# First layer pair of an MLP by Strassen's scheme for both batches, with the orders of two engines written out

## The chip, the cores and the metric

The kernel runs on one core of one Trainium2 chip. The metric is the device time of one execution in microseconds (us), as the median of the runs shown. PE is the matrix engine, DVE the vector engine, ACT the scalar engine, POOL the GpSimd engine, SP the engine that issues transfers.

## The reference

Clustered attention (2 batches, 8 heads, 768 rows of 64) feeds two MLPs, all in float32 on 1536 rows of 512:

```python
mask = q_assign[:, :, :, None] == k_assign[:, :, None, :]
scores = np.where(mask, scale * q @ k.T, -1e9)      # per head
attn = softmax(scores) ; x = attn @ v               # (2*768, 512)
h = x @ w_in ; g = h * sigmoid(h) ; x = g @ w_out   # MLP 1, d_ff 2048
gate = sigmoid(x @ w_gate) ; val = x @ w_val        # MLP 2, d_ff 1536
out = (gate * val) @ w_out
```

The weights come in as 64-bit floats and are converted in the kernel.

## The kernel before, in words

Attention goes through eight pairs of heads, four for each batch. For each pair PE forms the scores of 12 tiles of 128 rows, DVE takes their maxima, ACT the exponentials, PE transposes them and multiplies them by the values (`values`, L551). The last pair ends in `finish_last` (L630, L637): PE spreads the reciprocal denominators over the rows by matmuls with the identity, DVE multiplies them into the values and writes the quarter of the activations `acc`. For each batch `acc` has four quarters: b11 and b12 are ready before the last pairs, b21 and b22 only when the last pair's first and second half are finished.

MLP 1 works in eight pairs of 128-wide column blocks of `w_in` (`hidden`), each followed by its output product (`mixed`). A pair with four quarters of the activations is a 2x2 block product, done by Strassen's scheme in Winograd's form (`strassen`): seven products, named x, X, y, z, w, v, W, in place of eight. Their right operands are the quarters b11, b21, b22 and the sums t1 = b12 - b11, t2 = b22 - t1, t3 = b22 - b12, t4 = t2 - b21. X goes on in the PSUM bank of x, W in that of w; the difference d is read from w's bank before W goes on there. A product is KQ x 3 = 6 matmuls for a batch, since each float32 operand is split into a rounded high part (ACT, L65) and a low part (a subtraction, on DVE or POOL, L81 and L1003), and three of the four combinations are kept.

For the first pair the batches go apart. Batch 0 uses the scheme, its operands having been made long before. Batch 1 is done without it: `direct` forms eight products, 2 times 24 matmuls (L1013), from the four quarters. Its sums t1 to t4, which the later pairs need, are made after that (`right_sums`, `right_last`), while PE does the first output products.

The weights are converted in three DVE passes a chunk (L778, L780, L782; two, L775 and L782, where the lowest bits are kept too), with ACT before and POOL after them; a pair of input weights is two chunks, and POOL then builds the sums s1 to s4 (L827 to L830) and low parts (L807). The lists `behind` and `paced` hold instructions behind which the next passes (DVE) or the next copies (ACT) are queued.

What sets the order: a scheduler orders every engine's queue at build time. `tc.manual_schedule` makes the named engines take the traced order; around the first pair this holds for PE alone, so DVE's and ACT's orders there are the scheduler's. `tc.issue_after(ins)` puts the instructions of the block that are on `ins`'s own engine behind `ins` in its queue; it adds no wait between engines.

Of the kernel before, what the change touches and what calls it, by code (L numbers as in the profile page):

```python
# [32 lines left out]
def clustered_attention_then_two_mlps(ctx, tc, qT, kT, v, cen, cenT, w1i, w1o, w2g, w2v, w2o, out):  # L33
# [26 lines left out]
    copied, latest, moved, firsts, added = [], [], [], [], []  # L60
# [28 lines left out]
    def right_sums(temporary, name, b, caster, adder, kept):  # L89

        put = partial(right_operand, name, b, caster=caster, subber=adder)
        b11, b21, b12, b22 = quarters(b).values()
        t1 = temporary(f"{name}t1{b}")
        adder.tensor_tensor(t1, b12, b11, op=ALU.subtract)
        kept[b] = t1
        t2 = temporary(f"{name}t2{b}")
        adder.tensor_tensor(t2, b22, t1, op=ALU.subtract)
        put("t2", t2)
        yield
        t4 = temporary(f"{name}t4{b}")  # L100
        adder.tensor_tensor(t4, t2, b21, op=ALU.subtract)
        put("t4", t4)
        yield
        t3 = temporary(f"{name}t3{b}")
        adder.tensor_tensor(t3, b22, b12, op=ALU.subtract)
        put("t3", t3)
        yield

    def scheme_operands(temporary, name, b, caster, adder):
# [4 lines left out]
        def minus(n, x, y):  # L114
            sums[n] = temporary(f"{name}t{n}{b}")
            adder.tensor_tensor(sums[n], x, y, op=ALU.subtract)
# [20 lines left out]

    def right_last(name, b, src, caster, subber):
        right_operand(name, b, "t1", src, caster, subber)

    rp = ctx.enter_context(tc.tile_pool(name="rp", bufs=2))
    with ExitStack() as att:
# [404 lines left out]
        def values(p, j, g):  # L547
            vv = heads[p][4]
            o = ps_v.tile([P, G], F32, tag="v", name=f"v{p}_{j}_{g}")
            for n, kt in enumerate((4, 5, 0, 1, 2, 3)):  # L550
                m = nc.tensor.matmul(  # L551
                    o[(L, U)[kt % 2]],
                    lhsT=vv[:, j, kt, :],
                    rhs=ring[:, kt, g * G : (g + 1) * G],
                    start=n < 2,
                    stop=n >= NT - 2,
                )
            main, rest = (L, U) if j == 0 else (U, L)
            other = wk.tile([P, G], F32, tag="other", name=f"other{p}_{j}_{g}", bufs=1)
            ends[:] = [nc.scalar.activation(other[main], o[rest], AF.Copy), m]  # L560
            if p not in xf:
                xf[p] = fin.tile([P, S], F32, tag="xf", name=f"xf{p}")
            nc.vector.tensor_tensor(xf[p][main, g * G : (g + 1) * G], o[main], other[main], op=ALU.add)  # L563
# [54 lines left out]
        def finish_last(h):  # L618
# [9 lines left out]
            for j, r in enumerate((L, U)):  # L628
                for i in range(n):
                    nc.tensor.matmul(  # L630
# [5 lines left out]
                    )  # L636
            nc.vector.tensor_tensor(  # L637
                acc[:, hp, h, b, :], xf[p][:, h * HS : (h + 1) * HS], rb[:, 0:HS], op=ALU.mult
# [91 lines left out]
    up = ctx.enter_context(tc.tile_pool(name="up", bufs=8))  # L730
    home[1, "t1"] = ctx.enter_context(tc.tile_pool(name="tu", bufs=1))
# [135 lines left out]
    coming, ready = {}, {}  # L867

# [63 lines left out]
    def temporary(name):  # L932
        return up.tile([P, 2, HS], F32, tag="u", name=name)
# [3 lines left out]
    def strassen(w, name, take, bs, order="xyzwXvW"):  # L937

        def run(o, a, q, start=True):
            for k in range(KQ):  # L940
                for n, (s, t) in enumerate(((0, 0), (0, 1), (1, 0))):
                    for b in range(B)[bs]:
                        nc.tensor.matmul(  # L943
# [6 lines left out]
                        )  # L950
# [54 lines left out]
    def direct(w, name, take, b):  # L1005

        for m in range(2):
            o = bank(f"{name}_{b}{m}", (ppa, ppb)[m])
            for h in range(2):
                for r in range(2):  # L1010
                    for k in range(KQ):
                        for n, (s, t) in enumerate(((0, 0), (0, 1), (1, 0))):
                            nc.tensor.matmul(  # L1013
                                o[:, h, 0:HS],
                                lhsT=w[f"a{m + 1}{r + 1}"][s][:, k, :],
                                rhs=right[b, f"{r + 1}{h + 1}"][t][:, k, :],
                                start=r == 0 and k == 0 and n == 0,
                                stop=r == 1 and k == KQ - 1 and n == 2,
                            )
            take(o[:, :, 0:HS], m, b)  # L1020
            yield
# [9 lines left out]
    def hidden_directly(i, b):  # L1031
        def take(c, m, b):
            g = temporary(f"g{i}_{m}_{b}")
            nc.scalar.activation(g, c, AF.Silu)
            split(g, m, (slice(0, 2), b), f"a{i}", nc.vector)

        yield from direct(weights("1i", i), f"p{i}", take, b)
# [36 lines left out]
    def gated(i, bs, together=False):  # L1074
        gates = {}

        def gate(c, m, h, bs, inside):
            g = c if inside else temporary(f"g2{i}_{m}{h}{bs.start}")[:, bs]
# [3 lines left out]
        def value(c, m, h, bs, inside):  # L1082
# [7 lines left out]
            if together:  # L1090
                late[m, h] = parts
# [123 lines left out]
    kept = {}  # L1215
    ACT, DVE, POOL = nc.scalar, nc.vector, nc.gpsimd

    def sums(name, b):
        return right_sums(temporary, name, b, ACT, DVE, kept)

    def last(name, b):
        right_last(name, b, kept.pop(b), ACT, DVE)
# [18 lines left out]
    run(following)  # L1241
    weights("1o", 0, 1)
    rest = sums("x", 1)
    next(rest)
    with tc.issue_after(parted[0].ins):
        run(rest)
    last("x", 1)
    run(mixed(0, 0))
    run(mixed(0, 1))
    run(hidden(1, ALL))  # L1250
    for i in range(2, N1):
        following = hidden(i, ALL) if i < N1 - 1 else hidden(i, ONE[0], "xyzXwvW")
        steps(following, n=2 if i < N1 - 1 else 5)
        run(mixed(i - 1, first=int(i == N1 - 1)))
# [7 lines left out]
    zero, one = (scheme_operands(temporary, "y", b, ACT, DVE) for b in range(B))  # L1262
# [14 lines left out]
    subs = []  # L1277

    def rounding(m, h):
        late.pop((m, h))(subs)  # L1280

    def splitting():
        subs.pop(0)()

    def split_now(m, h):
        late.pop((m, h))()

# [4 lines left out]
    rounding(0, 0)  # L1292
    go(n=2)
    splitting()
# [9 lines left out]
    rounding(1, 0)  # L1304
    go(n=1)
    splitting()
    split_now(1, 1)
    go(n=1)
    rounding(0, 1)
    one("21")  # L1310
    splitting()
# [15 lines left out]
    rounding(0, 0)  # L1327
    go(n=2)
    splitting()
# [5 lines left out]
    rounding(1, 0)  # L1335
    go(n=1)
    splitting()
    split_now(1, 1)
    go(n=1)
    split_now(0, 1)  # L1340
# [81 lines left out]
```

## Time and profile before

| | |
|---|---|
| time, median of 3 runs | 768.25 us (767.39 to 768.47) |
| the profiled execution, its own time | 767.51 us |
| its span, first to last instruction | 765.7 us |
| busy in the span: PE, DVE, ACT, POOL | 755.2, 597.7, 425.9, 389.7 us |
| granted clock of PE | 1.000 of full speed |

The span is the time from the first to the last instruction on the core; the execution's own time is 1.8 us longer. Where a matmul's row gives a time, its end is modelled, and neighbouring rows overlap; the distance between starts tells the pace.

### The profile page before, as it was taken

To read this page: it belongs to the slowest core of one execution; us is meant where nothing else is said; L and a number is where in the kernel's file an instruction comes from. 1 tells how busy PE (TensorE), PEld (TensorE's weight loads), DVE (VectorE), ACT (ScalarE), POOL (GpSimd) and SP (SyncE) were. 2 spreads that over 40 slices of the span, in tenths; PEclk is the share of its full clock that TensorE was granted. 3 is DMA by queue.
4 is the path that set the end of the run, shared out by engine and by line. 5 is a ranking of instruction groups with operands and counts; after the bars stand their busy time and mean duration, and the time that the engine had idled before them with its cause. 6 is when DMAs were issued, how large, how long until landed. Compare 5 with 4: busy or idle time off the path is not lost.

```text
span 765.7 us, 11470 instructions
## 1 busy us (share of the span) xinstructions
PE 755.2 (99%) x4289; PEld 648.9 (85%) x4290; DVE 597.7 (78%) x773; ACT 425.9 (56%) x742; POOL 389.7 (51%) x361
## 2 busy tenths in 40 slices
PE   8999999999999999999999999999999999999997
PEld 4766776677767998998989989999999989999896
DVE  7887887788788968798978587986697767859566
ACT  6777776776886762534615545565544525353320
POOL 5235134644655773566647456125776745565430
PEclk9999999999999999999999999999999999999999
DMA  7677457447122122132222120010313112111104
GB/s 209 168 210 192 115 151 195 117 128 193 45 77 72 66 83 83 41 125 83 83 83 73 66 82 1 29 56 27 110 56 108 58 55 97 68 57 56 55 1 166
DMA packets 25488, 71.61 MB, mean 94 GB/s; under 512 B 4484, under 2 KB 4952, under 8 KB 25432
## 3 DMA queue, kind: packets, MB, share of 16 engines
q1 hardware_dynamic: 24888, 70.84, 30.7%
q8 instruction: 34, 0.56, 0.3%
q14 instruction: 22, 0.18, 0.1%
q10 hardware_dynamic: 544, 0.03, 0.0%
HBM read 48.01 MB, written 3.19 MB: 67 GB/s over the span
## 4 chain that ended last, share of the span: by engine, by line
PE 92%; DVE 3%; ACT 2%; DMA 1%; issue 1%; POOL 0%; SPq 0%; ACTq 0%
PE z L1134 13%; PE s L501 8%; PE v L551 7%; PE t L538 5%; PE y L1064 4%; PE h_0w L943 4%; PE h_0x L943 4%; PE v_0x L943 3%; PE g_0w L943 3%; PE g_0x L943 3%; PE v_0w L943 3%; PE y_00None L1064 2%; PE y_21None L1064 2%; PE y_20None L1064 2%; PE y_11None L1064 2%; PE y_10None L1064 2%
## 5 line engine op out<-in xcount | busy, mean ns | idle before, releaser
L514 ACT ACTIVATE e<-s,nm 128x768 f32<-128x768 f32 x96 | 86.5, 901 | 33.8 <-DVE nm L509 32.7
L509 DVE TENSOR_REDUCE nm<-s 128x1 f32<-128x768 f32 x96 | 91.4, 953 | 10.3 <-PE s L501 8.6
L1134 PE MATMUL z<-wu,ghb 128*128 128x512 f32 (+1 forms) x292 | 89.1, 387 | 0.0
L551 PE MATMUL v<-ph,vv 128*64 128x384 f32 x384 | 69.0, 495 | 0.1
L1134 PEld LDWEIGHTS z<-wu,ghb 128*128 128x128 f32 x292 | 54.5, 188 | 10.8
L501 PE MATMUL s<-ka,qa 128*128 128x384 f32 x192 | 57.5, 380 | 2.0 <-ACT e L514 1.5
L538 PE MATMUL t<-ident,e 128*128 128x128 f32 x384 | 58.4, 275 | 0.1
L1134 PE MATMUL z<-wu,glb 128*128 128x512 f32 (+1 forms) x146 | 56.7, 388 | 0.0
L538 PEld LDWEIGHTS t<-ident,e 128*128 128x128 f32 x384 | 44.9, 140 | 11.3 <-issue 9.0
L551 PEld LDWEIGHTS v<-ph,vv 128*64 128x64 f32 x384 | 24.7, 136 | 32.7 <-issue 29.0
L501 PE MATMUL s<-k,q 128*128 128x384 f32 x192 | 49.6, 339 | 0.0
L65 ACT ACTIVATE ph<-t 128x512 f32<-128x512 f32 x68 | 40.6, 598 | 12.6 <-PE t L538 12.0
L1043 DVE TENSOR_TENSOR acc<-z,acc 128x1024 f32<-128x1024 f32 x24 | 29.2, 1221 | 21.6 <-PE z L1134 21.6
L68 DVE COPY ph<-u 128x512 f32<-128x512 f32 x48 | 32.7, 682 | 16.3 <-PE u L528 16.3
L582 POOL TENSOR_TENSOR acc<-xf,rb 128x768 f32<-128x768 f32 x7 | 12.9, 1837 | 59.2 <-DMA rb<-d_rb 56.5
L807 POOL TENSOR_TENSOR wu<-cu,wu 128x512 fp32r<-128x512 f32 x12 | 16.3, 1356 | 52.0 <-ACT wu L65 52.0
L807 POOL TENSOR_TENSOR wo<-co,wo 128x512 fp32r<-128x512 f32 x16 | 24.1, 1510 | 33.5 <-ACT wo L65 33.4
L501 PEld LDWEIGHTS s<-k,q 128*128 128x128 f32 x192 | 34.5, 188 | 0.5 <-DMA k<-rows 0.3
L501 PEld LDWEIGHTS s<-ka,qa 128*128 128x128 f32 x192 | 28.9, 190 | 6.9 <-ACT e L514 5.9
L1064 PE MATMUL y<-gha,wo 128*128 128x384 f32 x128 | 32.8, 334 | 0.0
L1134 PEld LDWEIGHTS z<-wu,glb 128*128 128x128 f32 x146 | 27.4, 188 | 6.0 <-DVE glb L1003 0.5
L563 DVE TENSOR_TENSOR xf<-v,other 64x384 f32<-64x384 f32 x32 | 17.7, 553 | 14.8 <-ACT other L560 14.3
(709 smaller groups left out, 2151.9 us busy)
## 6 DMA issues: line engine op xcount, KB each, us to landing
ri<-in_w1i SPq DMA_DIRECT2D x16, 512.0 KB, 3.2
ro<-in_w1o SPq DMA_DIRECT2D x16, 512.0 KB, 3.1
ka<-kh SPq DMA_DIRECT2D x32, 192.0 KB, 3.6
rg<-in_w2g SPq DMA_DIRECT2D x12, 512.0 KB, 3.6
rv<-in_w2v SPq DMA_DIRECT2D x12, 512.0 KB, 3.1
ru<-in_w2o SPq DMA_DIRECT2D x12, 512.0 KB, 3.2
qq<-in_qT SPq DMA_DIRECT2D x8, 384.0 KB, 3.6
kk<-in_kT SPq DMA_DIRECT2D x8, 384.0 KB, 4.1
```

The source lines that it names most:

```text
L65: return nc.scalar.activation(o, i, AF.Copy)
L68: return nc.vector.tensor_copy(o, i)
L501: nc.tensor.matmul(s[:, g, 0:HS], lhsT=a[:, j, i * P : (i + 1) * P], rhs=c[:, j, g * HS : (g + 1) * HS], start=n == 0, stop=n == 1,)
L509: maxima.append(nc.vector.tensor_reduce(nm, s[:, :, 0:HS], axis=AX.XY, op=ALU.max, negate=True))
L514: x = nc.scalar.activation(e, s[:, :, 0:HS], AF.Exp, bias=nm, scale=1.0, accum_out=tots[p][:, n : n + 1])
L538: nc.tensor.transpose(t[:, kt, :], e[:, kt * P : (kt + 1) * P], ident)
L551: m = nc.tensor.matmul(o[(L, U)[kt % 2]], lhsT=vv[:, j, kt, :], rhs=ring[:, kt, g * G : (g + 1) * G], start=n < 2, stop=n >= NT - 2,)
L807: nc.gpsimd.tensor_tensor(lo, src, hi, op=ALU.subtract)
L943: nc.tensor.matmul(o[:, b, 0:HS], lhsT=w[a][s][:, k, :], rhs=right[b, q][t][:, k, :], start=start and k == 0 and n == 0, stop=k == KQ - 1 ...
L1043: added.append(nc.vector.tensor_tensor(z if to is None else to, o, z, op=ALU.add))
L1064: nc.tensor.matmul(o[:, d, 0:width], lhsT=s[:, d, k, :], rhs=t[:, c], start=k == 0 and m == 0, stop=k == 1 and m == 2,)
L1134: nc.tensor.matmul(o[:, a, c], lhsT=s[:, q * P : (q + 1) * P], rhs=r[:, c], start=k == 0 and m == 0, stop=k == 1 and m == 2, skip_group_ch ...
```

## The change

1. `finish_last` and `values` of the last pair: the queue of PE becomes value, denominators, value, denominators; the second value's PSUM tile comes from another pool (`ps_t`). The rounding of the first output weights is queued behind ACT's last copy of the ring (`drained`) and no longer behind the Silu table's load.
2. The first pair's batch 1 goes through `hidden(0, ONE[1], "xXyzwvW", True)`: seven products. `direct`, `hidden_directly`, `right_sums` and `right_last` go. The sums t1 to t4 of batch 1 are made by `scheme_operands`, between the products of batch 0. DVE's and ACT's orders are written out from batch 0's w to the last split of batch 1. The low parts of batch 0's hidden values are all on DVE and stand behind batch 1's products x to w; batch 1's (1, 1) quarter stays on POOL. Quarter 12 of batch 1 is no longer rounded. The DVE passes of pair 1's input weights are queued behind the last low part of batch 0 and behind batch 1's sum of v.
3. The first four DVE passes of the gate's weights are queued behind the last pair's sum of w (`sum_of_w`, the difference d of `hidden(7, ONE[0])`).
4. The pool of temporaries has seven shared buffers and one that only t1 and the values of X use (`own`).

```diff
-        for g in range(2):
-            values(p, 1, g)
-            if g == 0:
-                with tc.issue_after(ends[0].ins):
-                    moved[:] = [nc.scalar.activation(ex, unit[:, 0:1], AF.Silu)]
-            finish_last(g)
+        drained[:] = moved
+        values(p, 1, 0)
+        with tc.issue_after(ends[0].ins):
+            moved[:] = [nc.scalar.activation(ex, unit[:, 0:1], AF.Silu)]
+        with tc.issue_after(ends[1].ins):
+            finish_last(0)
+        with tc.issue_after(product[0].ins):
+            values(p, 1, 1, ps_t)
+        with tc.issue_after(ends[1].ins):
+            finish_last(1)
+        ends[1] = product[0]
...
+    own = ctx.enter_context(tc.tile_pool(name="own", bufs=1))
-    up = ctx.enter_context(tc.tile_pool(name="up", bufs=8))
-    home[1, "t1"] = ctx.enter_context(tc.tile_pool(name="tu", bufs=1))
+    up = ctx.enter_context(tc.tile_pool(name="up", bufs=7))
+    home[1, "21"] = ctx.enter_context(tc.tile_pool(name="tu", bufs=1))
...
-            job(("1o", i, e), plain, w1o[i, e], f"o{i}_{e}", () if i else moved)
+            job(("1o", i, e), plain, w1o[i, e], f"o{i}_{e}", () if i else (drained, moved)[e])
...
+                if c == place["2g", 0]:
+                    behind.extend(sum_of_w * 4)
...
-    def hidden(i, bs, order="xyzwXvW"):
+    def hidden(i, bs, order="xyzwXvW", apart=False):
         def take(c, m, h, bs, inside):
-            g = c if inside else temporary(f"g{i}_{m}{h}{bs.start}")[:, bs]
+            g = c if inside else temporary(f"g{i}_{m}{h}{bs.start}", own if i or bs.start else None)[:, bs]
             nc.scalar.activation(g, c, AF.Silu)
-            split(g, m, (h, bs), f"a{i}", nc.gpsimd if m and h else nc.vector)
+            helped = m and h and not (apart and bs.start == 0)
+            parts = partial(split, g, m, (h, bs), f"a{i}", nc.gpsimd if helped else nc.vector)
+            if apart:
+                late[bs.start, m, h] = parts
+            else:
+                parts()
...
-    for q in ("11", "12"):
-        right_quarter("x", 1, q, POOL, POOL)
-    for q in ("21", "22"):
-        right_quarter("x", 1, q, ACT, DVE)
-    front = hidden(0, ONE[0], "xwXyzvW")
-    steps(front, n=1)
+    right_quarter("x", 1, "11", POOL, POOL)
+    one = scheme_operands(temporary, own, "x", 1, ACT, DVE)
+    with tc.issue_after(finished[0].ins):
+        one("T1")
+    zeroth = partial(steps, hidden(0, ONE[0], "xwXyzvW", True))
+    zeroth(n=1)
     look[0] = AHEAD
     weights("1i", 0)
-    steps(front, n=5)
-    following = hidden_directly(0, 1)
-    next(following)
-    run(front)
-    run(following)
+    order.__exit__(None, None, None)
+    order = tc.manual_schedule(engines={mybir.EngineType.PE, mybir.EngineType.DVE, mybir.EngineType.Activation})
+    order.__enter__()
...
+    first = partial(steps, hidden(0, ONE[1], "xXyzwvW", True))
+    zeroth(n=1)
+    with tc.issue_after(ends[0].ins):
+        one("+21")
+    one("T2", "T3", "+t2", "+t3")
+    zeroth(n=1)
+    one("+t1", "21", "t2")
+    zeroth(n=1)
+    one("t3")
+    rounding(0, 0, 0)
+    zeroth(n=1)
+    one("t1")
+    first(n=1)
+    one("+22")
+    rounding(0, 1, 1)
+    zeroth(n=1)
+    one("T4", "+t4")
+    rounding(0, 1, 0)
+    paced.extend(rounded * 2)
+    zeroth(n=1)
+    one("t4")
+    rounding(0, 0, 1)
+    first(n=2)
+    one("22")
+    rounding(1, 0, 0)
+    first(n=2)
+    splitting(0, 0, 0)
+    splitting(0, 1, 0)
+    splitting(0, 0, 1)
+    splitting(0, 1, 1)
+    behind.extend(parted * 3)
+    first(n=1)
+    behind.extend(critical[-1:] * 3)
+    rounding(1, 1, 1)
+    first(n=1)
+    rounding(1, 1, 0)
+    rounding(1, 0, 1)
+    splitting(1, 0, 0)
+    splitting(1, 1, 1)
+    splitting(1, 1, 0)
+    splitting(1, 0, 1)
+    order.__exit__(None, None, None)
+    order = tc.manual_schedule(engines={mybir.EngineType.PE})
+    order.__enter__()
     weights("1o", 0, 1)
-    rest = sums("x", 1)
-    next(rest)
-    with tc.issue_after(parted[0].ins):
-        run(rest)
-    last("x", 1)
-    run(mixed(0, 0))
+    outs = mixed(0, 0)
+    with tc.issue_after(product[0].ins):
+        next(outs)
+    run(outs)
...
         steps(following, n=2 if i < N1 - 1 else 5)
+        if i == N1 - 1:
+            sum_of_w[:] = critical[-1:]
```

`one("T2")` makes a sum on DVE, `one("+t2")` its rounding on ACT, `one("t2")` its low part on DVE; `rounding(b, m, h)` is the rounding of a quarter of batch b's hidden values on ACT, `splitting` its low part.

## Rows read from the trace of the kernel before

**Rows 1.** the page's first part: busy us, share of the span, instructions

```profile
PE 755.2 (99%) x4289; PEld 648.9 (85%) x4290; DVE 597.7 (78%) x773; ACT 425.9 (56%) x742; POOL 389.7 (51%) x361
```

**Rows 2.** busy time by stage; columns: window, us, then busy us (instructions) by engine

```profile
238.20:253.20 15.00, 15.00 (x86) 14.58 (x85) 12.07 (x19) 10.23 (x19) 8.47 (x9) 1.00 0.21 71
```

**Rows 3.** PE's instructions in order of time: start us, us, line, out<-in, xcount

```profile
232.28 2.16 PE L551 MATMUL v<-ph,vv 128*64 128x384 f32 x12
234.27 1.75 PE L630 MATMUL rb<-ident,rs 128*64 128x128 f32 x24
236.14 2.16 PE L551 MATMUL v<-ph,vv 128*64 128x384 f32 x12
238.23 1.33 PE L943 MATMUL h_0w<-xt,wi0s 128*128 128x384 f32 x6
...
242.71 1.32 PE L943 MATMUL h_0v<-xt,wi0b 128*128 128x384 f32 x6
243.87 4.32 PE L1013 MATMUL p<-x,wi0a 128*128 128x384 f32 x24
...
249.07 4.32 PE L1013 MATMUL p<-x,wi0b 128*128 128x384 f32 x24
253.23 0.33 PE L1064 MATMUL y<-gha,wo 128*128 128x384 f32 x1
```

**Rows 4.** DVE in the same view; in brackets the idle time before an instruction

```profile
233.12 1.64 DVE L780 SCALAR_TENSOR_TENSOR co<-ro,co 128x512 int32<-128x512 int32 x1
...
235.53 0.56 DVE L563 TENSOR_TENSOR xf<-v,other 64x384 f32<-64x384 f32 x1
...
238.86 0.56 DVE L563 TENSOR_TENSOR xf<-v,other 64x384 f32<-64x384 f32 x1 [2.12 <-ACT other L560]
239.46 0.55 DVE L637 TENSOR_TENSOR acc<-xf,rb 128x384 f32<-128x384 f32 x1
...
242.91 0.95 DVE L81 TENSOR_TENSOR x<-acc,x 128x768 fp32r<-128x768 f32 x1
243.78 0.55 DVE L957 TENSOR_TENSOR h_0u<-h_0z,h_0u 128x384 f32<-128x384 f32 x1
244.25 0.55 DVE L1003 TENSOR_TENSOR gla<-g,gha 128x384 fp32r<-128x384 f32 x1
244.71 0.68 DVE L780 SCALAR_TENSOR_TENSOR ci<-ri,ci 128x512 int32<-128x512 int32 x1
...
247.78 1.18 DVE L782 SCALAR_TENSOR_TENSOR ci<-ri,ci 128x512 int32<-128x512 int32 x1
```

**Rows 5.** ACT in the same view

```profile
238.34 0.48 ACT L560 ACTIVATE other<-v 64x384 f32<-64x384 f32 x1 [0.76 <-PE v L551]
```

**Rows 6.** POOL in the same view

```profile
232.75 1.46 POOL L807 TENSOR_TENSOR wi0t<-si,wi0t 128x512 fp32r<-128x512 f32 x1
237.14 2.53 POOL L807 TENSOR_TENSOR wo<-co,wo 128x512 fp32r<-128x512 f32 x2 [2.93 <-ACT wo L65]
...
247.40 1.02 POOL L1003 TENSOR_TENSOR gla<-h_0d,gha 128x384 fp32r<-128x384 f32 x1 [6.21 <-ACT gha L65]
...
259.65 1.74 POOL L807 TENSOR_TENSOR wi1t<-si,wi1t 128x512 fp32r<-128x512 f32 x1
```

**Rows 7.** PE in the same view, MLP 1's pair 1

```profile
272.09 2.24 PE L943 MATMUL h_0y<-xt,wi1s 128*128 128x384 f32 x12
```

**Rows 8.** PE in the same view, MLP 1's last pair

```profile
443.46 1.20 PE L943 MATMUL h_0w<-xt,wi7s 128*128 128x384 f32 x6
445.09 0.50 PE L1064 MATMUL y_00None<-gha,wo 128*128 128x512 f32 x1 [0.43 <-DVE h_0u L957]
```

**Rows 9.** DVE in the same view, MLP 1's last pair and the output product

```profile
442.06 0.92 DVE L775 SCALAR_TENSOR_TENSOR cg<-cg,rg 128x512 int32<-128x512 int32 x1
...
444.49 0.55 DVE L957 TENSOR_TENSOR h_0u<-h_0y,h_0u 128x384 f32<-128x384 f32 x1
...
459.03 1.23 DVE L1043 TENSOR_TENSOR acc<-y_20None,acc 128x1024 f32<-128x1024 f32 x1 [1.50 <-PE y_20None L1064]
```

More of the change, by code (lines that the diff above doesn't have):

```diff
@@ L59, in clustered_attention_then_two_mlps @@
     maxima = []
-    copied, latest, moved, firsts, added = [], [], [], [], []
+    copied, latest, moved, drained, firsts, added, finished, product = [], [], [], [], [], [], [], []
     home = {0: xp}
@@ L87, in right_quarter, with scheme_operands @@
         right_operand(name, b, q, quarters(b)[q], caster, subber, "t1" if q == "12" else None)
[L89 to L109, printed above, removed]
+    def scheme_operands(temporary, own, name, b, caster, adder):
         b11, b21, b12, b22 = quarters(b).values()
@@ L114, in minus @@
         def minus(n, x, y):
-            sums[n] = temporary(f"{name}t{n}{b}")
+            sums[n] = temporary(f"{name}t{n}{b}", own if n == "t1" else None)
             adder.tensor_tensor(sums[n], x, y, op=ALU.subtract)
@@ L629, in finish_last @@
                 for i in range(n):
-                    nc.tensor.matmul(
+                    product[:] = [nc.tensor.matmul(
                         rb[r, i * P : (i + 1) * P],
@@ L867, in clustered_attention_then_two_mlps @@
     coming, ready = {}, {}
+    sum_of_w = []
     def come(*key, apart=False):
@@ L942, in run @@
                     for b in range(B)[bs]:
-                        nc.tensor.matmul(
+                        product[:] = [nc.tensor.matmul(
                             o[:, b, 0:HS],
@@ L1003, in split @@
         parted[:] = [subber.tensor_tensor(lo, src, hi, op=ALU.subtract)]
[L1005 to L1021, printed above, removed]
-    def hidden(i, bs, order="xyzwXvW"):
+    def hidden(i, bs, order="xyzwXvW", apart=False):
         def take(c, m, h, bs, inside):
-            g = c if inside else temporary(f"g{i}_{m}{h}{bs.start}")[:, bs]
+            g = c if inside else temporary(f"g{i}_{m}{h}{bs.start}", own if i or bs.start else None)[:, bs]
             nc.scalar.activation(g, c, AF.Silu)
-            split(g, m, (h, bs), f"a{i}", nc.gpsimd if m and h else nc.vector)
-        yield from strassen(weights("1i", i), f"h{i}", take, bs, order)
[L1031 to L1037, printed above, removed]
+            helped = m and h and not (apart and bs.start == 0)
+            parts = partial(split, g, m, (h, bs), f"a{i}", nc.gpsimd if helped else nc.vector)
+            if apart:
+                late[bs.start, m, h] = parts
+            else:
+                parts()
+        yield from strassen(weights("1i", i), f"h{i}", take, bs, order)
     def accumulate(z, o, first, to=None):
@@ L1077, in gate @@
         def gate(c, m, h, bs, inside):
-            g = c if inside else temporary(f"g2{i}_{m}{h}{bs.start}")[:, bs]
+            g = c if inside else temporary(f"g2{i}_{m}{h}{bs.start}", own if i else None)[:, bs]
             nc.scalar.activation(g, c, AF.Sigmoid)
@@ L1090, in value @@
             if together:
-                late[m, h] = parts
+                late[bs.start, m, h] = parts
             else:
@@ new lines, in splitting @@
+    def splitting(*key):
+        if key not in subs:
+            rounding(*key)
+        parted[:] = [subs.pop(key)[0]()]
+    first = partial(steps, hidden(0, ONE[1], "xXyzwvW", True))
[14 more added lines that the diff above has]
+    zeroth(n=1)
@@ L1261, in clustered_attention_then_two_mlps @@
     order.__enter__()
-    zero, one = (scheme_operands(temporary, "y", b, ACT, DVE) for b in range(B))
+    zero, one = (scheme_operands(temporary, own, "y", b, ACT, DVE) for b in range(B))
     rest = mixed(N1 - 1, 1)
@@ L1291, in clustered_attention_then_two_mlps @@
     parted_weights("2o", 0, 0)
-    rounding(0, 0)
+    rounding(0, 0, 0)
     go(n=2)
-    splitting()
+    splitting(0, 0, 0)
     zero("22")
@@ L1303, in clustered_attention_then_two_mlps @@
     go(n=4)
-    rounding(1, 0)
+    rounding(0, 1, 0)
     go(n=1)
-    splitting()
-    split_now(1, 1)
+    splitting(0, 1, 0)
+    splitting(0, 1, 1)
     go(n=1)
-    rounding(0, 1)
+    rounding(0, 0, 1)
     one("21")
-    splitting()
+    splitting(0, 0, 1)
     outs = out_of(0)
@@ L1326, in clustered_attention_then_two_mlps @@
     one("+22")
-    rounding(0, 0)
+    rounding(1, 0, 0)
     go(n=2)
-    splitting()
+    splitting(1, 0, 0)
     one("t4")
@@ L1334, in clustered_attention_then_two_mlps @@
     go(n=4)
-    rounding(1, 0)
+    rounding(1, 1, 0)
     go(n=1)
-    splitting()
-    split_now(1, 1)
+    splitting(1, 1, 0)
+    splitting(1, 1, 1)
     go(n=1)
-    split_now(0, 1)
+    splitting(1, 0, 1)
     critical.append(parted[0])
```

38 lines of the change are left out of this document (16 added, 22 removed).

## Prediction

> **What bounds the kernel now.** I read the engine totals first: the matrix engine is busy for 755.2 of 765.7 us [rows 1], so only its own instructions, and the moments in which it waits, can move the time. Then the table of the stretch that is rewritten, 238.2 to 253.2 us: PE 15.00 of 15.00 us busy, vector engine (DVE) 12.07 of 15.00 [rows 2]. PE has no gap there, but DVE has only 3 us to spare, and it has to take on new work. Next the matmuls one after the other [rows 3], then what feeds them on DVE [rows 4], ACT [rows 5] and POOL [rows 6], and last the one wait that PE shows between 262 us and the end phase, at 445 us [rows 8].
>
> Two readings are used throughout. A busy PE is not PE at its pace: 24 matmuls of 384 columns run from 249.07 to 253.23, 4.16 us, so one takes 0.173 us and a set of six (one of Strassen's products for one batch) 1.04 us. A set that starts after a wait takes 1.16 (242.71 to 243.87) [rows 3]: a wait costs its length and 0.12 more. And on DVE two independent instructions overlap by 0.09: a 768-wide subtraction shows 0.95, but the next starts 0.87 after it (242.91 to 243.78) [rows 4]; a 384-wide one shows 0.55, so 0.46. Where one needs the other, it starts 0.04 after the other's end.
>
> **Attention's end.** The order was value, both groups of denominators, value; it becomes value, denominators, value, denominators. The 24 records of the denominators start at 234.27; their row lasts 1.75 with about 0.27 for the last one, so one is issued each (1.75 - 0.27) / 23 = 0.064 us and the 24 are through at 235.8. The second value starts only at 236.14, because the one PSUM buffer is empty when DVE's addition ends, 235.53 + 0.56 = 236.09 [rows 3, 4]. In the new order the second value has another buffer. A value takes 1.99 (232.28 to 234.27). So: 234.27 + 12 x 0.064 = 235.04, second value until 237.1, 0.77 for the second denominators, the set w at 237.95 instead of 238.23: 0.3 us gained. The last quarter of the activations, b22, ended at 239.46 + 0.55 = 240.01 [rows 4]. Now the denominators end last, near 238.0; ACT's copy of half a value (0.48 [rows 5]) and DVE's addition (0.56 [rows 4]) follow the value's end at 237.2 to 238.4, and DVE's product ends near 239.0.
>
> **Seven products in place of eight.** Batch 1 of the first pair had 2 x 24 = 48 matmuls and gets 7 x 6 = 42: 6 x 0.173 = 1.04 us less on PE. From w to the first matmul of the output product PE went through 14 sets in 253.23 - 238.23 = 15.00 us, 14 x 1.04 = 14.56 and 0.44 of waits. With 13 sets and no wait the output product would start at 237.95 + 13.52 = 251.5.
>
> **What DVE has to do for it.** The sums t1 to t4 of batch 1 stood after 253 us, where nobody waited. Now they stand between. DVE's order is written out; I walk it with the durations above. T1 needs only old quarters and fits between DVE's product at 236.7 and the second value: DVE was idle for 2.12 us there [rows 4]. From 239.0: T2 until 239.95, T3 240.8, low part of 21 241.7, of t2 242.55, y's sum 243.05, low part of t3 243.9, z's sum 244.4, difference d 244.95. PE meanwhile: w 237.95, X 239.0, y 240.0, z 241.1, batch 1's x 242.15, v 243.3, and W would start at 244.35. But W goes on in the bank that d is read from, so it waits until 245.0: 0.65 + 0.12 lost. Further on DVE: low part of t1 245.85, v's sum 246.3, T4 247.15, W's sum 247.65. The low part of t4 needs ACT's rounding of T4, which stands behind three other ACT instructions and ends near 248.3, so 249.3; y's sum of batch 1 249.8, low part of 22 250.65, z's sum 251.1, d 251.7. PE: X 246.2, y 247.2, z 248.25, w 249.3, v 250.35, and its W, which waits for that d in the same way, at 251.75 rather than 251.4: 0.35 + 0.12 lost. It ends at 252.9, and the output product starts there (its first low part on DVE ends at 252.2). **0.3 us gained over 253.23**, where PE alone would give 1.7. Of the 1.4 lost, 1.24 are these two waits and the rest a short wait of batch 1's x for its bank.
>
> A price that could differ is DVE beside POOL. DVE's pass at 233.12 took 1.64 us while POOL computed a low part (232.75, 1.46) [rows 4, 6]; the same kind of pass took 0.68 at 244.71. Up to 247.4 POOL was idle for 6.2 us [rows 6], so the new sums mostly run alone; at the ends they may meet POOL's low part of the output weights and its clamps of the next pair's weights. Bounds: nothing, or one such loss at either end, 2 x 0.95 less what the waits absorb, so up to 1.2; I take nothing, since the subtractions of 242.91 and 244.25 us stood at 0.95 and 0.55 with POOL idle [rows 4].
> The Trainium skill ("SBUF — State Buffer", "Who interferes with whom") says that a DVE instruction with two SBUF inputs and a GpSimd instruction that reads SBUF exclude each other, the later one being blocked until the first ends. The 1.64 us pass agrees: it ended 0.55 after POOL's instruction. By that rule T1, if it comes second to POOL's low part (1.26 us each), would be up to 1.3 later, and the sum below would lose as much.
>
> **What moves behind it.** The six DVE passes of pair 1's input weights are tied behind the last split of batch 0 and behind batch 1's v sum. The last one ended at 247.78 + 1.18 = 248.96; now four splits end near 253.6, the six passes of about 0.5 us each follow with two sums of batch 1 between them, so near 258 at the latest. Behind it POOL builds Strassen's sums: the low part of s1 and s2 ended at 259.65, where the last one starts, so 10.7 us after the passes [rows 4, 6]. It is wanted at 272.09 by pair 1's product y [rows 7], at 271.8 after the change. From 258 it ends at 268.7, 3 us early: no cost. ACT's two copies for these weights follow a rounding of batch 0 and delay no set. POOL's dropped rounding of quarter 12, one rounding of output weights ahead of the Silu table, the buffers (seven shared and one own in place of eight) cost nothing: each has a reader several us later.
>
> **Gate's passes.** At 445.09 PE waited 0.43 us for DVE's sum of y, 444.49 + 0.55 = 445.04, which stood behind two passes of the gate's weights (the first of them at 442.06, 0.92) [rows 8, 9]. With the passes behind the sum of w, y's sum ends near 443.5, and the product starts when the set at 443.46 is through, 444.5: 0.43 of waiting and 0.12 of refill, 0.55. The passes then run between the output product's additions, where DVE is idle for 1.5 us at a time [rows 9]; the gate's weights are wanted 40 us later.
>
> **Sum.** 0.3 + 0.55 = 0.85 us less than the profiled execution's 767.51 (span 765.7), 766.65. The median of the runs shown is 768.25, 0.74 above that execution, so 767.4. About 0.2%, 1.5 us, is what a measurement of this kernel can tell from no change.
>
> **Rivals.**
> *DVE is not late.* If b22 comes earlier or the sums overlap more, PE alone sets the start, 251.5 to 251.9: 1.7 to 1.35 gained, with the gate 2.25 to 1.9: 766.0 to 766.3. For it: two waits of half a microsecond hang on a chain of eight DVE instructions. Against it: DVE's 12 us of work stood in 15 already. 0.28.
> *DVE is later still.* T1 falls behind the second value (0.95), or meets POOL at both ends (1.2): most of it reaches W, so 0.1 to 0.6 more than before in all, 768.4 to 768.9. 0.17.
> *Pair 1's weights come late; slower.* If the last DVE pass ends after 261.1 (271.8 - 10.7), PE waits at pair 1's second product, a microsecond for each. Six passes beside POOL at 1.2 to 1.6 us, queued behind four more splits, would end near 265: 3.9 lost, 771.3. Against it: DVE's sums that filled 253 to 266 are gone. 0.10.
> *The change does not bite at 445 us*, since another DVE instruction takes the passes' place: 768.0, inside the forecast's own range.
>
> **How the numbers follow.** Forecast 0.45 (767.0 to 768.0), rivals 0.28, 0.17, 0.10. Faster by over 0.2% (below 766.7): the first rival and a sliver of the forecast, 0.31. Slower (above 769.8): the third, 0.10 and a little of the second, 0.11. Within: 0.58. The range goes from the first rival's end to the second's, 765.9 to 769.0.
>
> **What would show it.** In the profile after: batch 1's W of the first pair with a wait on d, as batch 0's W; the output product starting at 252.9; no wait at the seventh output product. Wrong would be a gap ahead of pair 1's second product, or PE without any wait from 238 to 252.

## The result and the profile after

The changed kernel takes 772.31 us (median of 6 runs, 771.71 to 772.88) beside 768.25 (6 runs, 767.39 to 768.75): a ratio of 1.0054, 95% interval 1.0041 to 1.0067. It is slower by 4.1 us, and outside the range. The profiled execution took 771.71, its span 769.9, 4.2 more than before; PE is busy for 755.8 us, as before [rows 1]. Landmarks of PE place the 4.2:

| stretch | before | after | difference |
|---|---|---|---|
| first instruction to the first product x of MLP 1 | 230.63 | 231.21 | +0.58 |
| x to the first output product | 22.60 | 23.95 | +1.35 |
| from there to pair 2's x | 31.34 | 31.21 | -0.13 |
| pair 2's x to its z | 20.52 | 23.84 | +3.32 |
| from there to the last pair's first output product | 140.00 | 139.41 | -0.59 |
| from there to the end | | | -0.33 |

The first line moves without the change: among the experiments on the kernel before, the same x stood at 230.73 to 231.58. The table of PE's waits after the change (us in total, times, longest) names the rest:

```profile
PE h_0y L933 <- POOL wi2s L794: 2.3, 1, 2.3
...
PE h_1x L933 <- ACT g L998: 0.7, 1, 0.7
...
PE h_0w L933 <- DVE h_0d L947: 0.5, 1, 0.5
...
PE h_1w L933 <- DVE h_1d L947: 0.3, 1, 0.3
PE h_0y L933 <- DVE acc L618: 0.3, 1, 0.3
...
PE y_20None L1033 <- DVE acc L1012: 0.3, 1, 0.3
```

The wait of 445 us [rows 8] is gone and four waits stand in the first pair (0.7, 0.5, 0.3, 0.3). The largest wait, for POOL's `wi2s`, belongs to pair 2: no step of the prediction looked at it. The first pair in PE's order of time (start us, us, line, out<-in, xcount, idle before and its releaser), which answers to [rows 3]:

```profile
238.49 1.31 PE L933 MATMUL h_0w<-xt,wi0s 128*128 128x384 f32 x6
...
241.15 1.33 PE L933 MATMUL h_0y<-xt,wi0s 128*128 128x384 f32 x6 [0.30 <-DVE acc L618]
...
244.26 1.31 PE L933 MATMUL h_1x<-x,wi0a 128*128 128x384 f32 x6 [0.73 <-ACT g L998]
...
247.14 1.34 PE L933 MATMUL h_0w<-x,wi0t 128*128 128x384 f32 x6 [0.52 <-DVE h_0d L947]
...
254.00 1.32 PE L933 MATMUL h_1w<-x,wi0t 128*128 128x384 f32 x6 [0.32 <-DVE h_1d L947]
255.16 0.34 PE L1033 MATMUL y<-gha,wo 128*128 128x384 f32 x1
```

What feeds it, DVE and then POOL:

```profile
235.33 1.64 DVE L769 SCALAR_TENSOR_TENSOR co<-ro,co 128x512 int32<-128x512 int32 x1
237.01 0.56 DVE L543 TENSOR_TENSOR xf<-v,other 64x384 f32<-64x384 f32 x1
237.67 0.55 DVE L618 TENSOR_TENSOR acc<-xf,rb 128x384 f32<-128x384 f32 x1
238.14 1.70 DVE L96 TENSOR_TENSOR xtt<-acc 128x768 f32<-128x768 f32 x1
239.88 0.56 DVE L543 TENSOR_TENSOR xf<-v,other 64x384 f32<-64x384 f32 x1
240.54 0.55 DVE L618 TENSOR_TENSOR acc<-xf,rb 128x384 f32<-128x384 f32 x1
```

```profile
234.71 1.72 POOL L794 TENSOR_TENSOR wo<-co,wo 128x512 fp32r<-128x512 f32 x1
237.75 1.28 POOL L794 TENSOR_TENSOR wo<-co,wo 128x512 fp32r<-128x512 f32 x1 [1.33 <-ACT wo L65]
```

Two DVE instructions run beside POOL's two low parts and take 1.64 and 1.70 us: the third pass (L769) and T1 (L96). In [rows 4] a subtraction of T1's size took 0.95, and the same pass of before took 0.71:

```profile
234.79 0.71 DVE L782 SCALAR_TENSOR_TENSOR co<-ro,co 128x512 int32<-128x512 int32 x1
```

T1 stands ahead of the last quarter's addition and product in DVE's queue, so the last quarter is ready at 241.09. The walk had it near 239.0, which is 239.6 in this execution, whose x is 0.58 later: 1.5 us late.

The wait at pair 2, from its loads on. The loads of raw weights, of before and then of after (start us of the first, us):

```profile
246.87 2.49 SPq L756 DMA_DIRECT2D ro<-in_w1o  x2
264.61 5.58 SPq L756 DMA_DIRECT2D ri<-in_w1i  x2
```

```profile
260.58 0.93 SPq L743 DMA_DIRECT2D ro<-in_w1o  x2
270.20 4.19 SPq L743 DMA_DIRECT2D ri<-in_w1i  x2
```

There are two raw buffers, and a load starts when the last DVE pass over the chunk before has left one: before, the pass at 246.12 ended at 246.80 and the load came at 246.87; after, the passes of L769 from 259.82 free it for 260.58. That load is of output weights, 13.7 us later than before. Pair 2's input weights use the buffers after them: their load is 5.6 us later, 3.8 when the 1.8 us later x of pair 2 is taken off. At the end of that chain POOL makes the low part wi2s (POOL's order of time, before and then after), and PE's product y of after waits for it (third fence):

```profile
284.06 1.32 POOL L807 TENSOR_TENSOR wi2s<-si,wi2s 128x512 fp32r<-128x512 f32 x1
```

```profile
290.47 1.27 POOL L794 TENSOR_TENSOR wi2s<-si,wi2s 128x512 fp32r<-128x512 f32 x1
```

```profile
288.56 0.96 PE L933 MATMUL h_0y<-xt,wi2s 128*128 128x384 f32 x4
291.79 1.66 PE L933 MATMUL h_0y<-xt,wi2s 128*128 128x384 f32 x8 [2.27 <-POOL wi2s L794]
```

Before, wi2s ended at 285.38 and y began one set of twelve (2.08) behind x (284.57), at 286.65, so 1.27 us later. The first four matmuls of y (0.69) use the rounded high part alone, as the third fence shows: only the fifth waits for the low part. So the slack was 1.96 us. After, wi2s ended 5.37 behind x instead of 0.81: 4.56 later, 2.60 more than the slack, and y's fifth matmul started 2.65 late. The 4.56 are 3.2 by which the last pass over these weights ended later, and 1.3 that POOL lost behind it, as two of its instructions there (at 286.38 and 288.39) took 1.46 and 1.43 beside DVE, and 0.75 each before. Each weight buffer's reader has its own slack, and this one was not looked up.

### The profile page after: what moved, and what is told of

Read it like the earlier page. It is cut to its first block, busy times and chain, and to the rows that moved or that the text cites. A ratio compares the mean times of both kernels' runs of the same rounds, so it can differ in the third digit from the quotient of the medians.

```text
span 769.9 us, 11472 instructions
## 1 busy us (share of the span) xinstructions
PE 755.8 (98%) x4283; PEld 648.2 (84%) x4284; DVE 603.0 (78%) x780; ACT 428.3 (56%) x747; POOL 381.8 (50%) x359
## 4 chain that ended last, share of the span: by engine, by line
PE 88%; DVE 5%; ACT 3%; issue 2%; POOL 1%; DMA 1%; SPq 0%; DVEq 0%; ACTq 0%; POOLq 0%
PE z L1103 13%; PE s L478 8%; PE v L531 7%; PE t L515 5%; PE y L1033 4%; PE v_0x L933 3%; PE g_0w L933 3%; PE g_0x L933 3%; PE h_0w L933 3%; PE v_0w L933 3%; PE h_0x L933 3%; PE y_20None L1033 2%; PE y_21None L1033 2%; PE y_00None L1033 2%; PE y_11None L1033 2%; PE y_10None L1033 2%
## 5 line engine op out<-in xcount | busy, mean ns | idle before, releaser
L794 POOL TENSOR_TENSOR wo<-co,wo 128x512 fp32r<-128x512 f32 x16 | 22.2, 1390 | 22.4 <-ACT wo L65 22.4
```

What stands on the lines that cost most here:

```text
L794: nc.gpsimd.tensor_tensor(lo, src, hi, op=ALU.subtract)
```

## The experiments

All times beside runs of the kernel before on the same chip (767.96 to 768.37 in the medians). "Behind x" is the time from the first x of MLP 1 to the first output product: 22.60 before, 23.95 after.

**The parts alone.** The gate's passes behind the sum of w, on the kernel before:

```diff
+                if c == place["2g", 0]:
+                    behind.extend(sum_of_w * 4)
...
+        if i == N1 - 1:
+            sum_of_w[:] = critical[-1:]
```

> The kernel before with part 3 alone: the first four DVE passes of the gate's weights are queued behind the last pair's sum of w. Theory: the wait of 0.43 us at the seventh output product goes, with its refill 0.55 us, and nothing else changes: 767.7 us. Rival: the passes only move the wait to a later instruction (the gate's weights or a bank of the output product): 768.2 to 768.6 us.

767.06 us, 0.9987 (0.9978 to 0.9995). The median is 1.3 us below the kernel before where 0.55 was expected; the interval reaches from 0.4 to 1.7. In the profiled execution the span is 0.7 shorter, 0.59 of it in the stretch with the gate's passes. The first pair is as before; the last pair's output product follows its set on PE without a wait, which was 0.43 us in [rows 8]:

```profile
443.59 1.20 PE L946 MATMUL h_0w<-xt,wi7s 128*128 128x384 f32 x6
444.63 0.39 PE L1067 MATMUL y_00None<-gha,wo 128*128 128x512 f32 x1
```

The reverse, the changed kernel without that tie:

```diff
-                    behind.extend(sum_of_w * 4)
```

> The changed kernel without part 3. Theory: the wait at the seventh output product is back, 0.55 us more than the changed kernel: 772.9 us. Rival: part 3 gives nothing here because its passes stand in the way later (the changed kernel waits 0.3 us for an addition at an output product): 772.3 us.

772.88, 1.006 (1.0047 to 1.0074). The 0.4 us wait is back, and from pair 2's z to the last pair's first output product it is 140.02, where the changed kernel has 139.41. In the traces part 3 does what was forecast, in both directions; the medians alone don't tell 0.6 us apart.

Attention's end alone (part 1), on the kernel before:

```diff
+        drained[:] = moved
+        values(p, 1, 0)
...
+        with tc.issue_after(product[0].ins):
+            values(p, 1, 1, ps_t)
...
+            job(("1o", i, e), plain, w1o[i, e], f"o{i}_{e}", () if i else (drained, moved)[e])
```

> The kernel before with part 1 alone: value, denominators, value, denominators at attention's end and the earlier rounding of the first output weights. Theory: the set w of the first pair starts 0.3 us earlier after batch 0's x than before (7.3 us behind it instead of 7.6), 767.9 to 768.0 us. Rival: the reordering is a part of the loss, since the set x started 0.58 us later in the changed kernel: 768.6 us or more.

769.12, 1.0013 (1.0004 to 1.0022). The set w starts 7.25 behind x instead of 7.60, the 0.3 us forecast, and the output product 23.86 behind it. On DVE:

```profile
235.83 1.64 DVE L790 SCALAR_TENSOR_TENSOR co<-ro,co 128x512 int32<-128x512 int32 x1
...
242.24 0.96 DVE L81 TENSOR_TENSOR x<-acc,x 128x768 fp32r<-128x768 f32 x1 [2.23 <-ACT x L65]
243.12 0.42 DVE L786 TENSOR_SCALAR ci<-ci 128x512 int32<-128x512 int32 x1
243.45 0.95 DVE L81 TENSOR_TENSOR x<-acc,x 128x768 fp32r<-128x768 f32 x1
244.32 0.55 DVE L965 TENSOR_TENSOR h_0u<-h_0y,h_0u 128x384 f32<-128x384 f32 x1
```

PE's product v waits 1.6 us for that last sum. The expectation was missed and its rival (768.6 or more) came. Two causes were open: the pass beside POOL's low part (the earlier rounding moved POOL there), and the scheduler's new order, in which y's sum stands behind two low parts and a pass. Before, it stood right behind the first low part, ahead of the second one (rows left out of [rows 4]):

```profile
241.23 0.96 DVE L81 TENSOR_TENSOR x<-acc,x 128x768 fp32r<-128x768 f32 x1 [1.22 <-ACT x L65]
242.11 0.55 DVE L957 TENSOR_TENSOR h_0u<-h_0y,h_0u 128x384 f32<-128x384 f32 x1
```

So part 1 without the earlier rounding, together with part 3:

```diff
-            job(("1o", i, e), plain, w1o[i, e], f"o{i}_{e}", () if i else (drained, moved)[e])
+            job(("1o", i, e), plain, w1o[i, e], f"o{i}_{e}", () if i else moved)
```

> The kernel before with the new order at attention's end (without the earlier rounding of output weights, so POOL's first low part of them stays behind the Silu table) and with the gate's passes behind the sum of w. If the 1.64 us pass beside POOL was the whole loss of the end alone: that pass takes 0.71 again, the raw buffer is refilled 0.93 us earlier, ACT doesn't wait for the load, and y's sum is 1.0 earlier; v still waits some 0.65 us, since the order of DVE's queue is that of the end alone (low part, pass, low part, then y's sum): output product 22.85 behind x instead of 23.86, and with the gate 768.0. If the new order itself gains its 0.3 us: 22.3 behind x, 767.3. If the queue's order is the loss and not the pass: 23.8, 768.9.

767.77, 0.9996 (0.9986 to 1.0005); 23.39 behind x. On DVE:

```profile
235.70 0.69 DVE L790 SCALAR_TENSOR_TENSOR co<-ro,co 128x512 int32<-128x512 int32 x1
...
243.70 0.55 DVE L968 TENSOR_TENSOR h_0u<-h_0y,h_0u 128x384 f32<-128x384 f32 x1
```

The pass is short again, and the wait of v falls from 1.64 to 1.14 only: 0.5 us is the pass. The rest goes with the order of DVE's queue, which is argued from the rows: the new attention end with the old DVE order was not tried. None of the three places expected for the output product (22.85, 22.3 and 23.8) was met.

**The first pair.** T1 of batch 1 on POOL, at 205 us, in the changed kernel:

```diff
-    with tc.issue_after(finished[0].ins):
-        one("T1")
+    one("T1")
...
-            adder.tensor_tensor(sums[n], x, y, op=ALU.subtract)
+            (nc.gpsimd if name == "x" and n == "t1" else adder).tensor_tensor(sums[n], x, y, op=ALU.subtract)
```

> The changed kernel with the sum T1 computed by POOL, right behind quarter 11's rounding and some 25 us earlier, so that DVE doesn't meet POOL's second low part with it. Theory (the stage's loss is DVE blocked beside POOL; T1 took 1.70 us in place of 0.95 and stood ahead of the second half's product): the output product starts 22.3 us behind batch 0's x in place of 23.95, pair 2's wait of 2.3 us stays, 770.7 us. Rival (the chain of DVE's sums is too long by itself, T1 or not): 23.5 us or more behind x, 772 us.

770.58, 1.0032 (1.0019 to 1.0044); 22.51 behind x, 1.44 earlier than the changed kernel. On DVE:

```profile
235.12 1.65 DVE L769 SCALAR_TENSOR_TENSOR co<-ro,co 128x512 int32<-128x512 int32 x1
...
238.23 0.56 DVE L543 TENSOR_TENSOR xf<-v,other 64x384 f32<-64x384 f32 x1 [0.21 <-ACT other L540]
238.89 0.55 DVE L618 TENSOR_TENSOR acc<-xf,rb 128x384 f32<-128x384 f32 x1
```

The pass still takes 1.65, but with T1 away, its own 0.95 included, the last quarter follows the copy of its value; the waits of 0.73 and 0.30 are gone, and those for d stay (0.52, 0.34). The other half of the collision, the earlier rounding given up:

```diff
-            job(("1o", i, e), plain, w1o[i, e], f"o{i}_{e}", () if i else (drained, moved)[e])
+            job(("1o", i, e), plain, w1o[i, e], f"o{i}_{e}", () if i else moved)
```

> The changed kernel with both roundings of the first output weights behind the Silu table, as before, so that POOL's first low part comes some 2 us later. Theory: DVE's third pass at 235 us takes 0.7 again in place of 1.64 and the first half's product is 0.9 us earlier, but both low parts then stand beside T1 and T2, so most of it is lost again: the output product 23.5 to 24 us behind x, 772 to 772.4 us. Rival (the early rounding is the whole loss of the stage): 22.5 us behind x, 770.9 us.

772.35, 1.0052 (1.0038 to 1.0066); 23.22 behind x. POOL's low parts move to 237.59; the pass takes 0.69 and T1 0.95, at 237.03, but now T2 (239.83) meets POOL. On DVE:

```profile
235.17 0.69 DVE L769 SCALAR_TENSOR_TENSOR co<-ro,co 128x512 int32<-128x512 int32 x1
...
237.03 0.95 DVE L96 TENSOR_TENSOR xtt<-acc 128x768 f32<-128x768 f32 x1
...
239.83 1.36 DVE L96 TENSOR_TENSOR xtt<-acc,xtt 128x768 f32<-128x768 f32 x1
```

The 0.73 won in the first pair don't show in the time: pair 2's wait stayed, and in the profiled execution the clock fell behind it (last section).

**Pair 2's weights.** The passes of pair 1's input weights without their ties:

```diff
-    paced.extend(rounded * 2)
...
-    behind.extend(parted * 3)
...
-    behind.extend(critical[-1:] * 3)
```

> The changed kernel without the ties of pair 1's weights: their two ACT copies and six DVE passes are queued where the scheduler puts them, five of the passes ahead of batch 1's sum of y. Theory (late weights cost 2.4 us at pair 2's product y, because each later load waits for a buffer that pair 1's passes free): that wait goes, and the six passes, some 3 us of DVE's time, make the output product start 1.5 to 3 us later; 771.5 to 773 us in all. Rival (the 2.3 us wait has another cause, as POOL's order): the wait stays and the first pair gets slower, 774 us or more.

771.82, 1.0047 (1.0034 to 1.0059). PE's wait for wi2s is gone and pair 2 takes 20.52 again, but six passes between the sums put the output product 27.11 behind x, 3.16 later: the waits for d and for v's bank grow to 1.6, 1.0 and 0.7. So the theory held, with 3.16 a little over its 1.5 to 3. What the ties save in one place they cost in the other.

Then the passes placed by hand, three behind the first split and three behind batch 1's W:

```diff
-    paced.extend(rounded * 2)
+    pair1 = begun([flat(w1i[2 + n]) for n in range(2)], "i1", False)
...
     splitting(0, 1, 0)
+    done1 = [result(pair1[0])]
...
-    behind.extend(parted * 3)
...
-    behind.extend(critical[-1:] * 3)
...
     first(n=1)
+    done1.append(result(pair1[1]))
```

> The changed kernel with pair 1's six DVE passes written into DVE's order: three behind batch 0's second split, three behind batch 1's sum of W, in place of after 257 us. Theory (each later load waits for one of two raw buffers that the passes free, so pair 2's weights come as late as pair 1's passes): the passes end 2 to 3 us earlier, pair 2's wait of 2.3 us shrinks to under 0.7, the first pair itself is unchanged; 770 us. Rival (pair 2's weights are late through POOL's own order): the wait stays at 2 us or more, 772 us.

771.28, 1.0044 (1.0031 to 1.0056): the wait falls from 2.3 to 1.7, not to under 0.7, though the load of pair 2 is issued 18.8 us ahead of pair 2's x where the changed kernel has 16.2 and the kernel before 20.0. With T1 on POOL as well:

> The changed kernel with T1 on POOL and with pair 1's passes written into DVE's order, both edits together. Theory: the two losses are separate and their removal adds up, the output product 22.3 us behind x and no wait over 0.7 us at pair 2: 768.0 to 769.0 us. Rival: the earlier start asks for pair 2's weights earlier by as much, so the wait at pair 2 is back with 1.5 us or more: 770 us.

769.80, 1.0023 (1.001 to 1.0036); 22.50 behind x, the wait 1.7: the rival's time and wait. Each remedy acts by itself and within the intervals they add up, but the kernel before stays ahead. Earlier still, three passes ahead of the low part of t4 and three behind the first split, against the kernel with both edits (its ACT copies are queued earlier too, by the line of `pair1`):

```diff
+    pair1 = begun([flat(w1i[2 + n]) for n in range(2)], "i1", False)
     one("+t1", "21", "t2")
...
-    pair1 = begun([flat(w1i[2 + n]) for n in range(2)], "i1", False)
     zeroth(n=1)
+    done1 = [result(pair1[0])]
     one("t4")
...
     splitting(0, 1, 0)
-    done1 = [result(pair1[0])]
+    done1.append(result(pair1[1]))
...
-    done1.append(result(pair1[1]))
```

> The changed kernel with T1 on POOL, and the six passes of pair 1's input weights earlier still: three before the low part of t4, three right behind the first split. If pair 2's weights are late only by when these passes free the raw buffers: the last one ends near 255 instead of 260.35, the first load is issued near 249 instead of 255.90, the next pair's near 264.5 instead of 266.68, and PE's wait of 1.7 us for POOL's wi2s is gone; the three passes (1.8 us) ahead of the low part of t4 cost the first pair 0.5 to 1.2 (output product 23.0 to 23.7 behind x). 768.3 to 769.0. If the lateness comes from POOL's own queue (its low parts and sums in the order traced) and not from the raw buffers: a wait of about 1.7 stays, 770.3 to 771.

769.79, 1.0021 (1.0012 to 1.003). The loads are issued at 250.31 and 263.64, and pair 2 takes 20.52: the wait is gone, by the place of pair 1's weights alone. But the output product stands 24.72 behind x, more than the 23.0 to 23.7 expected. DVE, then POOL, then PE:

```profile
251.49 1.98 DVE L114 TENSOR_TENSOR x<-acc,x 128x768 fp32r<-128x768 f32 x1
```

```profile
251.38 1.28 POOL L794 TENSOR_TENSOR wi1a<-ci,wi1a 128x512 fp32r<-128x512 f32 x1 [6.18 <-ACT wi1a L65]
```

```profile
254.65 1.31 PE L933 MATMUL h_1w<-x,wi0t 128*128 128x384 f32 x6 [1.66 <-DVE h_1d L947]
```

The earlier passes let POOL start its low part earlier, and that one falls on a low part of DVE's chain: 1.98 instead of 0.95, and batch 1's W waits 1.66 instead of 0.34. What pair 2 wins (22.46 to 20.52), the first pair loses (22.50 to 24.72), and the time doesn't change. Of the 2.22 lost, 1.03 is this collision; the expectation gave the passes alone 0.5 to 1.2. So pair 2's weights were late because pair 1's passes were; earlier passes also let POOL begin earlier, so this run doesn't part the raw buffers from POOL's queue. No place for the passes was found that is free for both pairs.

Last, a third raw buffer. There is no room for it unless MLP 2 gives up one of its weight buffers:

```diff
-rp = ctx.enter_context(tc.tile_pool(name="rp", bufs=2))
+rp = ctx.enter_context(tc.tile_pool(name="rp", bufs=3))
...
-NSP, MORE = 7, 3
+NSP, MORE = 7, 2
```

> The changed kernel with three raw buffers for the incoming weights in place of two (one buffer of rounded weights that only MLP 2 uses is given up for the room). Theory (a load starts when a pass frees a raw buffer, so the late passes of pair 1 delay the loads of its output weights and of pair 2): the loads run ahead, pair 2's wait of 2.3 us is gone or under 0.5 us while pair 1's passes stay where they are; the first pair is unchanged; 769.5 us if MLP 2 doesn't miss its buffer. Rival (DVE's and POOL's queues, not the loads, make pair 2's weights late): the wait stays at 1.5 us or more.

> The changed kernel with T1 on POOL and three raw buffers. Theory: both losses go, the output product 22.5 us behind x and no wait at pair 2: 767.3 to 768 us, level with the kernel before with part 3 alone. Rival: the wait at pair 2 is back with 1.5 us or more, 769.5 us.

> The changed kernel with T1 on POOL, pair 1's passes written into DVE's order as in the run before, and three raw buffers. Theory: passes and loads are both early, no wait at pair 2: 767.0 to 767.8 us. Rival: the passes between the splits push batch 0's second half of the output product, 768.5 us or more.

> The kernel before with part 3 alone and three raw buffers: what the buffer that MLP 2 gives up costs where no load was late. Theory: nothing is late for loads in the kernel before, so the time is that of part 3 alone, 767.1 to 767.5 us, or up to 1 us more if MLP 2 misses the buffer. Rival: earlier loads help elsewhere, 766.5 us or less.

In the changed kernel 776.08, with T1 on POOL 775.24, with the passes placed too 775.04; the kernel before with part 3 and the third buffer, as the control, 775.04 (ratios 1.0103, 1.0091, 1.0092, 1.0089): all four expected times were missed. The wait for wi2s falls with the third buffer from 2.3 to 1.0, with T1 on POOL to 0.5, and with both other edits it is gone. So the raw buffers carry a part of the lateness, more than half of that wait. The 1.0 that is left isn't the loads': with the third buffer pair 2's input weights are asked for 24.6 us ahead of pair 2's x, earlier than before (20.0). In that run the passes of the output weights follow pair 1's without a gap, and POOL's low part of batch 1 takes 5.98 us beside them, where it took 1.09 in the changed kernel:

```profile
258.71 5.98 POOL L1211 TENSOR_TENSOR gla<-h_1d,gha 128x384 fp32r<-128x384 f32 x1 [3.81 <-ACT gha L65]
```

How much of the 1.0 hangs on this was not tested. The control stands 6.8 us above the kernel before, where part 3 alone stood 1.3 below it, and the three edits with it are at the same 775.04; the giving up of that buffer costs more than is at stake. The control isn't free of waits in the first pair either: its first output product waits 1.4 us for a low part. MLP 2 then waits for its weights in all four (PE's waits with all three edits; 1.6 and 1.3 in the control), and behind these waits the clock falls (last section):

```profile
PE v_0y L933 <- ACT wv0s L65: 1.7, 1, 1.7
PE v_0y L933 <- POOL wv0s L794: 1.3, 1, 1.3
```

The best version of all is the smallest, part 3 alone: 767.06 us, where the kernel before took 768.37 beside it, 0.05 to 0.22% faster.

## Why the prediction was wrong

*Attention's end*: right on PE (w 7.28 behind x, 7.60 before). The end of the denominators set nothing; the last quarter, forecast near 239.0, came 1.5 us late for DVE's sake.

*Seven products on PE*: right. From w to the output product 16.67 us go by: 13 sets of 1.04 are 13.52, and the four sets that wait start 0.47, 0.90, 0.69 and 0.49 late, with some 0.12 behind each and behind the first set (2.55 + 0.6).

*The walk along DVE*: its order, its durations and its two waits held. The rest of it is only shifted: d ended at 247.09, which is the walk's 244.95 and the 0.58 and 1.5 us above; W of batch 0 started 0.69 late where 0.65 was forecast, batch 1's 0.49 where it was 0.35. The 0.90 of batch 1's x, for which the walk had 0.16, comes of the late quarter: with T1 away it is 0.09. With T1 away the output product came 22.51 behind x; the walk had 252.9 - 230.63 = 22.27. The forecast that DVE eats most of the 1.7 us was right.

*DVE beside POOL*: **the first step that failed.** It was bounded by 1.2 and taken at nothing, because the subtractions of 242.91 and 244.25 ran with POOL idle. But the nearest row for T1's place was the pass of 233.12, beside POOL; [rows 6] had POOL's two low parts of the output weights from 237.14 to 239.67, over the very time that T1 was given; and the change itself moved the first of them onto a pass, by rounding the output weights earlier. After the change the pass took 0.93 and T1 0.75 more than alone, and the last quarter came 1.5 late. With T1 away, its own 0.95 included, the output product came 1.44 earlier: the walk had room for T1 itself, so this is about what the collisions cost, where nothing was taken. The Trainium skill's rule ("SBUF — State Buffer", "Who interferes with whom") that the prediction quoted and did not follow would have given up to 1.3. The trace agrees: T1, begun 0.39 us behind POOL's instruction, ended 0.81 after that one's end (239.84, 239.03). The rival "DVE later still" named this place, with 0.1 to 0.6 more than before in all; the first pair lost 1.35.

*Pair 1's weights*: right that no wait stands there, though all came later: the passes ended at 261.10 (forecast 258 at the latest, and 261.1 was the limit that the rival gave for a wait). POOL's low part for pair 1's second product ended at 269.58, 8.5 behind the passes where 10.7 was taken, and 4.3 us before that product (273.89). **The second step that failed** is the words "no cost": only the first reader of the moved passes was followed. The passes also free the raw buffers, through which the next output weights and then pair 2's input weights come, and they hold back POOL's work behind them. There the slack was 1.96 us and the lateness 4.56. It cost 2.27 us of waiting and 3.32 in all. That the passes' place is the cause is shown (the two runs that put the passes earliest, without the ties and by hand, have no such wait); how it divides between buffers and POOL's queue is shown only so far as the third buffer takes the wait from 2.3 to 1.0. The rival "pair 1's weights late" came near the time (771.3) with the wrong place: its own test, a gap ahead of pair 1's second product, did not show. The time came from a wait one pair later.

*Gate's passes*: right, 0.55 forecast, 0.59 between the landmarks.

*Sum*: 0.85 less was forecast, 4.2 more came. Of these 5.05, the first pair is 1.35 + 0.3 = 1.65, pair 2 3.32; what is left, 0.1, are the small terms of the table. Pair 2's 3.32 are 2.76 by which its output product began late (the wait of 2.27 and the slower matmuls at both its ends) and 0.56 at y_20, which waited for an addition that DVE ended at 304.58, behind three passes of the next input weights. That this is the same lateness handed on fits the runs in which the wait is gone, which have no wait at y_20, but was not tried by itself.

## What to carry to other kernels

Whoever moves a conversion step should follow each of its outputs: the data, the buffer it frees, the load that waits for that buffer, and that load's reader, each with its own slack; the first reader's comfort says nothing of the next. And a step on one of two engines that block each other (here DVE and POOL) is to be laid out on one time line with the other engine's instructions, after the change and not before it: a collision cost the later one the remainder of the other's instruction (T1 ended 0.81 us after POOL's, a low part 0.81 after POOL's in the run with the earliest passes), and undoing it at one place put it at another.

## What was not expected of the hardware

After the 2.3 us wait PE's granted clock fell in some executions. Busy time by stretch in the changed kernel without the gate's tie (window, us, then busy us (instructions) of PE, PEld, DVE, ACT, POOL; PE's clock, DMA share, GB/s):

```profile
290.00:292.00 2.00, 0.00 (x0) 0.00 (x0) 1.06 (x1) 1.98 (x4) 2.00 (x4) 1.00 0.00 0
292.00:293.00 1.00, 0.98 (x6) 0.98 (x6) 1.00 (x2) 0.00 (x0) 1.00 (x1) 1.00 0.03 8
293.00:294.00 1.00, 1.00 (x6) 0.90 (x6) 0.97 (x2) 0.00 (x0) 1.00 (x2) 0.73 0.07 16
294.00:295.00 1.00, 1.00 (x4) 0.81 (x3) 1.00 (x1) 0.00 (x0) 0.67 (x1) 0.50 0.00 0
295.00:296.00 1.00, 1.00 (x4) 0.81 (x3) 0.97 (x3) 0.02 (x1) 0.00 (x0) 0.50 0.00 0
296.00:298.00 2.00, 2.00 (x8) 1.58 (x8) 2.00 (x3) 0.61 (x1) 1.30 (x1) 0.78 0.49 139
```

PE worked again when the clock went to half, 1.2 of 2.4 GHz, for some 3 us. From pair 2's x to its z this execution took 24.88 where the changed kernel's took 23.84 at full clock in the same windows: here a wait of 2.3 us cost 1.0 more. The kernel without the earlier rounding shows the same 24.88, with 0.50 from 292 to 294; the profiled kernels without this wait ran pair 2 in 20.5. In the runs with the third buffer the same follows MLP 2's two waits: from 500 to 505 us the clock stands at 0.68 with all three edits and at 0.71 in the control. Among the six times of the changed kernel, the mean clock was 0.997 for 772.81 and 772.88 and 0.999 for 771.71 and 771.88, so its median holds some of this too.
